# Two ScalarE passes for one of VectorE's in eight early slots, masks on GpSimd, and output pairs from slot 8, in a fused attention and SMELU kernel

## The chip, the cores and the metric

The kernel runs on one core of one Trainium2 chip. The metric is the device time of one execution in microseconds; the time of a kernel is the median of its runs.

## What is computed

Sliding-window attention over 8 batches, 8 heads, 576 positions and head size 64 gives 4608 rows of 512; these go through a feed-forward layer of width 2048 with the SMELU activation.

```python
scores = (q @ k.T) / sqrt(64)                       # kept where |i - j| <= 32
attn   = softmax(scores) ;  x = attn @ v            # x: [4608, 512]
h = x @ w_in                                        # w_in: [512, 2048]
g = h if h >= 1 else 0 if h <= -1 else (h + 1)**2 / 4
out = g @ w_out                                     # w_out: [2048, 512]
```

The kernel uses a form of g without branches. With rr = relu((h + 1)/2), g = min(rr, 1) * max(h, rr). The changed kernel has a second form of it, g = min(max(h, 1), rr * rr), since rr * rr is (h + 1)^2/4 for h over -1 and is at least h everywhere.

## The kernel before, in words

The feed-forward layer is cut into 18 row blocks of 256 rows (TB) by 8 column blocks of 256 hidden columns, in all 144 slots, numbered a in the loop at L462: t is the row block, f the column block. A slot does this, in the order of the code, which is the order in every engine's queue (the schedule is written by hand, L73):

- TensorE makes the hidden block hp in PSUM by 8 matmuls of 128x128 by 256 (L484). It reads xT, the attention's transposed output, and w_in. Slots 6 and 7 take their hp from the pool of the output tiles (L479), all others from ps_h, which has two buffers.
- ScalarE writes rr by a Relu (L488), VectorE writes mx by a max of hp and rr (L490) and gT by min and multiply (L491). hp is free when the max is done.
- run(a) (L498) does the attention work that the dictionary ev has for this slot; then come the output matmuls of `post` (L499), and run(a + 0.5) for attention work that stands behind them.

Output matmuls of the first two row blocks go by pairs (L432): a pair is 8 matmuls of 256 columns, two row tiles by four of the 16 column blocks, and eight pairs fill the output columns of one half. Which slots have which pair is the list `pairs` (L374) up to pair 7; after that slot a takes number a - 8 (L465). From number 16 on it is a quarter (L417), 4 matmuls of 512 columns, as long as a pair in TensorE time. ScalarE copies a finished output tile to osb (L429, L445), and SyncE stores it.

Attention is done per batch and ahead of its rows. `tposes` (L319) transposes q and k of batches 1 and 2 on TensorE into PSUM tiles, two of them per call; ScalarE and VectorE each copy a part of each out (L186). `scores` (L207) makes the scores, ScalarE takes their Exp (L231). The band mask is put in either by matmuls of a bias ahead of the scores (add_mask, L199), if eng is None, which is so below slot 14 (L464), or by a multiplication with mask4 or mask8 on VectorE after the Exp (L197). `sums` (L261) multiplies by v and by ones; ScalarE makes the reciprocal by Ln and Exp (L295, L296), and VectorE's multiplication (L301, L304) puts the result into xT. ps_s and ps_n, the PSUM pools of scores and sums, have one buffer each. `seq` holds the steps of batches 1 to 7, and `at` lays them on slots (L395 to L406). Row block 2 (slots 16 to 23) is the first that reads rows of batch 1.

mask4 and mask8 are copied from band on VectorE at slot 10 (L493). Loads are issued by GpSimd in the order of the code (L121 to L151): w_in in column pieces, then w_out's column half 0 in two row halves, q, k and v of batch 1, w_out's column half 1, and batch 2. In the built program each of GpSimd's loads waits for the one eight before it.

Of the kernel before, what the change touches and what calls it, by code (L numbers as in the profile page):

```python
# [9 lines left out]
AF = mybir.ActivationFunctionType  # L10
ALU = mybir.AluOpType
# [3 lines left out]
def kernel(  # L15
# [21 lines left out]
    NT, DM, DFF = out.shape[0], 512, 2048  # L37
# [4 lines left out]
    TAIL = S - MAIN  # L42
# [13 lines left out]
    ps_s = ctx.enter_context(tc.tile_pool(name="ps_s", bufs=1, space=bass.MemoryType.PSUM))  # L56
# [7 lines left out]
    band = const.tile([128, 192], BF, name="band")  # L64
    bias = const.tile([128, 192], BF, name="bias")
    mask4 = const.tile([128, 8 * 128], BF, name="mask4")
    mask8 = const.tile([128, 4 * TAIL], BF, name="mask8")
# [6 lines left out]
    V, P, A = nc.vector, nc.gpsimd, nc.scalar  # L74


    qn, kn, vn = {}, {}, {}

    def load_half(half, t, h, eng=None, x=None):

        src, dst, nm = ((q, qn, "qh"), (k, kn, "kh"))[t]
        if (0, half) not in dst:
            dst[0, half] = early.tile([128, 2, S], BF, name=nm, tag=nm, bufs=2) if x is None else x
        (eng or nc.gpsimd).dma_start(out=dst[0, half][:, h], in_=src[0].rearrange(
            "(h y) (l p j) d -> h l p y (j d)", h=2, l=2, p=32)[h][half])
# [7 lines left out]
    def load_nat(b, t):  # L93
        src, dst, nm = ((q, qn, "qn"), (k, kn, "kn"))[t]
        x = dst[b] = nat.tile([128, NU, 2, D], BF, name=nm, tag=nm)
        for h in range(2):
            nc.gpsimd.dma_start(out=x[:, :, h], in_=src[b, NY * h:NY * h + NY].rearrange("y s d -> (y s) d")  # L97
                                .rearrange("(u p) d -> p u d", p=128))

    def load_v(b, n):  # L100
        if b not in vn:
            vn[b] = nat.tile([128, 2 * NC, 2, D], BF, name="vn", tag="vn", bufs=3)
        h, a = divmod(n, 2)
        y = NY * h + 2 * a
        nc.gpsimd.dma_start(out=vn[b][64 * a:64 * a + 64, :, h], in_=v[b, y:y + 2].rearrange("y s d -> (y s) d")  # L105
                            .rearrange("(c r) d -> r c d", r=64))
# [35 lines left out]
    def put(todo):  # L142
        for fn, *x in todo:
            fn(*x)

    w = [(load_w_in, c, c + 256, h) for c in range(0, 1024, 256) for h in range(2)]
    w += [(load_w_in, c, c + 512, h) for c in range(1024, DFF, 512) for h in range(2)]
    put(w[:4] + [(load_half, 1, t, h) for t in range(2) for h in range(2)] + w[4:])
    put([(load_w_out, 0, n) for n in range(2)] + [(load_rows, 1, t) for t in range(2)])
    put([(load_v, 1, n) for n in range(4)] + [(load_w_out, 1, n) for n in range(2)])  # L150
    put([(load_rows, 2, t) for t in range(2)] + [(load_v, 2, n) for n in range(4)])  # L151
# [4 lines left out]
    def qkT(b, t):  # L156
# [2 lines left out]
        if b not in kT:  # L159
            kT[b] = ktp.tile([128, NY * S], BF, name="kT")  # L160
        return kT[b]

    HD = (slice(0, 64), slice(64, 128))

    def tpose(b, n, t, copy, ps):

# [13 lines left out]
        for j in range(j0, j1):  # L180
            if isinstance(src, list):
                for h in range(2):
                    nc.tensor.transpose(ps[HD[h], j - j0], src[h][:, D * j:D * j + D], ident)  # L183
            else:
# [3 lines left out]
    def xpose(b, t):  # L188

        nc.sync.dma_start_transpose(out=qkT(b, t).rearrange("d (u p) -> d u p", p=128),  # L190
                                    in_=(qn, kn)[t][b].rearrange("p u h d -> p (u h d)"))
# [7 lines left out]
    def add_mask(ps, n, w):  # L199
        for a in range(2):  # L200
            for h in range(2):
                nc.tensor.matmul(ps[h][HD[a], :n * w].rearrange("p (n j) -> p n j", n=n), ident[HD[h], HD[h]],
                                 bias[HD[h], 64 * h:64 * h + w].rearrange("p (n j) -> p n j", n=1)
                                 .to_broadcast([64, n, w]),
                                 start=True, stop=False, skip_group_check=True)

    def scores(b, ys, pars, cs, eng, pool=ps_s):  # L207
# [8 lines left out]
        for y1 in range(*ys):  # L216
            for par in range(*pars):
                for c2 in range(*cs):
                    c = 2 * c2 + par
                    for a in range(2):  # L220
                        for h in range(2):
                            s0 = S * (y1 + 2 * a) + 64 * c
                            nc.tensor.matmul(ps[HD[a], h, 128 * n:128 * n + 128], kT[b][HD[h], s0:s0 + 64],  # L223
                                             qTs[b % 3][HD[h], PAD + s0 - 32:PAD + s0 + 96],
                                             start=eng is not None, stop=True, skip_group_check=True)
# [8 lines left out]
    def scores8(b, eng, pool=None):  # L234
# [9 lines left out]
        for y1 in range(2):  # L244
            for a in range(2):
                for h in range(2):
                    s0 = S * (y1 + 2 * a) + MAIN
                    nc.tensor.matmul(ps[h][HD[a], TAIL * y1:TAIL * y1 + TAIL], kT[b][HD[h], s0 + 32:s0 + TAIL],
                                     qTs[b % 3][HD[h], PAD + s0:PAD + s0 + TAIL],
# [57 lines left out]
    def flush():  # L307
        while muls:
            muls.pop(0)()
# [61 lines left out]

    NB = NT // TB
    NF = DFF // 256
    pairs = [(10, 0), (10, 1), (11, 2), (12, 3), (13, 4), (14, 5), (15, 6), (16, 7)]  # L374
    ev = {}

    def at(a, *todo):


        ev.setdefault(a, []).extend(x for x in todo if x)  # L380

    def steps(b, cut):

        for k, (lo, hi) in enumerate(((0, cut), (cut, MAIN))):
            for y1 in range(2):
                yield (sums, b, y1, lo, hi), (scores, b, (y1, y1 + 1), (0, 2), (2 * k, 2 * k + 2))
        yield (sums, b, 0, MAIN, S), (scores8, b)
# [4 lines left out]
    at(4, (sums, 0, 1, TB, MAIN))  # L392
    at(5, (sums, 0, 0, MAIN, S, ps_s))
    seq = [x for b in range(1, B) for x in steps(b, 224)]
    at(15, seq[0][0], (*seq[1][0], ps_s))  # L395
    for n, a in enumerate((18, 20, 22, 27)):
        at(a, seq[2 + n][0])
    for n, a in enumerate((13.5, 14.5, 16, 18, 20, 25, 27)):
        at(a, seq[n][1])
    sl = [30, 32, 35, 39, 42, 45, 49, 52, 56, 59, 62, 65, 69, 73, 77, 81, 84, 88, 92]  # L400
    sl += [96, 99, 103, 106, 110, 113, 116, 120, 124, 128]
    for n, a in enumerate(sl):
        at(a, seq[6 + n][0], seq[7 + n][1] if n < len(sl) - 1 else None)
    for b, *a in ((1, 11.5, 12.5), (2, 19.5, 21.5)):
        for t in range(2):
            at(a[t], (tposes, b, (t, 0), (t, 1)))  # L406
    loads, xps = {}, {}
    for b in range(LONG, B):
        a = sl[5 * (b - 1) - 7] - 17
# [5 lines left out]
    gT, op = {}, {}  # L415
# [33 lines left out]
    def run(pos):  # L449
        todo = []  # L450
        for fn, *x in ev.get(pos, []):
            if fn is sums:
                todo.append(sums(*x))
            elif fn is tposes:
                tposes(*x)
            else:
                pool = (x.pop(),) if x[-1] in (ps_s, ps_n, ps_o) else ()
                fn(*x, eng, *pool)
        for end in todo:
            end()  # L460

    for a in range(NF * NB + NF):  # L462
        t, f = divmod(a, NF)
        eng = None if a < 14 else V  # L464
        post = [x for n, x in pairs if n == a] + [a - NF] * (a >= 2 * NF)  # L465
        for b, x in loads.get(a, []):
            if x < 2:
                load_nat(b, x)
            else:
                for n in range(4):  # L470
                    load_v(b, n)
        if a == 0 or a > 3:
            flush()
        if t < NB:
            if t not in gT:
                gT[t] = gtp.tile([128, 2 * NF, TB], BF, name="gT", tag="gT")
            r0 = TB * t % RING
            if a in (6, 7):
                hp = ps_o.tile([128, 2, TB], FP, name="hp", tag="op")  # L479
            else:  # L480
                hp = ps_h.tile([128, 2, TB], FP, name="hp", tag="hp")
            for j in range(2):
                for n, kk in enumerate((0, 2, 1, 3)):
                    nc.tensor.matmul(hp[:, j], w_in[:, kk, 256 * f + 128 * j:256 * f + 128 * j + 128],  # L484
                                     xT[:, kk, r0:r0 + TB], start=n == 0, stop=n == 3)

            rr = ewp.tile([128, 2, TB], FP, name="rr")
            A.activation(rr, hp, AF.Relu, scale=0.5, bias=0.5)  # L488
            mx = ewp.tile([128, 2, TB], FP, name="mx")
            V.tensor_max(mx, hp, rr)  # L490
            V.scalar_tensor_tensor(gT[t][:, 2 * f:2 * f + 2], rr, 1.0, mx, op0=ALU.min, op1=ALU.mult)  # L491
        flush()
        if a == 10:  # L493
            for h in range(2):
                for m, n, w in ((mask4, 8, 128), (mask8, 4, TAIL)):
                    V.tensor_copy(m[HD[h]].rearrange("p (n j) -> p n j", n=n), band[HD[h], 64 * h:64 * h + w]
                                  .rearrange("p (n j) -> p n j", n=1).to_broadcast([64, n, w]))
        run(a)  # L498
        for x in post:  # L499
            (pair if x < 4 * 4 else quarter)(x)  # L500
        run(a + 0.5)
        for x in xps.get(a, []):
            xpose(*x)
# [30 lines left out]
```

The softmax here doesn't subtract the row's maximum and nothing guards it: scores larger than these inputs give would overflow.

## Time and profile before

The three runs took 316.71, 316.87 and 317.66 us; the median is 316.87. The profiled run has a span of 315.0 us.

| what | before |
|---|---|
| TensorE matmuls, busy | 298.4 us, 95% |
| VectorE, busy | 250.8 us, 80% |
| ScalarE, busy | 192.1 us, 61% |
| hidden matmuls L484 | 149.3 us busy in 1152 |
| output matmuls L424, L440 | 123.0 and 16.3 us busy in 477 and 128 |
| Relu L488, mean | 595 ns |
| max L490 and multiply L491, mean | 690 and 692 ns |
| mask copies on VectorE, L496 | 1.19 us from 35.40 us |
| chain of waits that ended last | 86% TensorE, 5% VectorE, 5% ScalarE |

The profile is of one execution. Times count from the start of the span. Engines are PE (TensorE's matmuls), PEld (its weight loads, beside them), DVE (VectorE), ACT (ScalarE), POOL (GpSimd) and SP (SyncE). In the timeline a row is a start, a duration, the engine, the line, the operation with its tiles, and in brackets the idle time ahead of it and what ended that. The ends of matmuls are modelled, so that consecutive ones overlap in the rows; start-to-start times are the safer ones. An instruction that waits for several things is put down to one of them, and where the engine named had long been done it was another.

### The profile page before, as it was taken

How to read it: one execution, taken by the hardware profiler on the slowest of the kernel's cores; microseconds unless marked ns; L12 is line 12 of the kernel's file. 1: busy time of each engine (PE TensorE's matmuls, PEld its weight loads, DVE VectorE, ACT ScalarE, POOL GpSimd, SP SyncE). 2: the span in 40 equal slices, each digit the busy share in tenths (PEclk: the TensorE clock that was granted, in tenths of full speed). 3: DMA queues.
4: the chain of work that ended last, by engine and by line, in shares of the span. 5: the costliest groups of instructions: out<-in, count | busy, mean ns of one | idle time of the engine just before them, and what ended most of it. 6: DMA issues, size and time to landing. Idle time of an engine off the chain costs nothing.

```text
span 315.0 us, 8563 instructions
## 1 busy us (share of the span) xinstructions
PE 298.4 (95%) x3670; PEld 207.7 (66%) x3707; DVE 250.8 (80%) x393; ACT 192.1 (61%) x316; POOL 69.5 (22%) x83
## 2 busy tenths in 40 slices
PE   8987998999999999999999999999999999999995
PEld 3566877776666666666666666666666666667652
DVE  4279986877988888888888888888888888878760
ACT  3677375765765776567756666566676666654431
POOL 8784354652060406040503000000000000000000
PEclk9999999999999999999999999999999999999999
DMA  9999999999999969997993983005501100100111
GB/s 151 185 199 202 174 215 174 164 169 166 168 167 117 107 141 167 101 91 123 173 127 54 90 127 95 33 35 111 108 35 35 36 33 35 36 33 35 42 60 67
DMA packets 123558, 34.54 MB, mean 110 GB/s; under 512 B 108160, under 2 KB 119168, under 8 KB 123520
## 3 DMA queue, kind: packets, MB, share of 16 engines
q0 software_dynamic: 94176, 18.06, 74.1%
q1 hardware_dynamic: 29200, 15.63, 19.7%
q8 instruction: 29, 0.48, 0.6%
q10 hardware_dynamic: 144, 0.29, 0.4%
q14 instruction: 9, 0.07, 0.1%
HBM read 36.70 MB, written 9.44 MB: 146 GB/s over the span
## 4 chain that ended last, share of the span: by engine, by line
PE 86%; DVE 5%; ACT 5%; issue 3%; ACTq 0%
PE hp L484 37%; PE op L424 35%; PE bb L289 5%; PE op L440 4%; PE bb L223 2%; PE z L332 2%; DVE mx L490 2%; ACT pt L231 1%; ACT rc L296 1%; DVE gT L491 1%; PE tp L183 1%; DVE xT L301 1%; ACT lr L295 1%; DVE kT L186 1%; DVE qT L186 1%
## 5 line engine op out<-in xcount | busy, mean ns | idle before, releaser
L484 PE MATMUL hp<-xT,w_in 128*128 128x256 bf16 x1152 | 149.3, 273 | 4.0 <-DVE mx L490 1.9
L488 ACT ACTIVATE rr<-hp 128x512 f32<-128x512 f32 x144 | 85.7, 595 | 92.5 <-PE hp L484 91.1
L484 PEld LDWEIGHTS <-w_in 128*128 128x128 bf16 x1152 | 111.8, 98 | 44.2 <-issue 5.0
L424 PE MATMUL op<-w_out,gT 128*128 128x512 bf16 x477 | 123.0, 379 | 5.0 <-issue 4.8
L490 DVE TENSOR_TENSOR mx<-hp,rr 128x512 f32<-128x512 f32 x144 | 99.3, 690 | 33.7 <-ACT rr L488 31.5
L491 DVE SCALAR_TENSOR_TENSOR gT<-rr,mx 128x512 bf16<-128x512 f32 x144 | 99.6, 692 | 4.9
L424 PEld LDWEIGHTS <-gT 128*128 128x128 bf16 x512 | 47.6, 98 | 36.7
L231 ACT ACTIVATE pt<-bb 128x1024 bf16<-128x1024 f32 (+1 forms) x33 | 33.2, 1012 | 5.4 <-PE bb L223 4.0
L105 POOL DMA_DIRECT2D vn<-in_v_dram x32 | 27.3, 867 | 40.7 <-PE bb L223 36.2
L301 DVE TENSOR_TENSOR xT<-bb,rc 128x512 bf16<-128x512 f32 (+1 forms) x32 | 21.1, 658 | 11.1 <-ACT rc L296 10.4
L429 ACT COPY osb<-op 128x512 f32<-128x512 f32 x32 | 18.7, 583 | 11.5 <-PE op L424 11.1
L296 ACT ACTIVATE rc<-lr 128x512 f32<-128x512 f32 (+2 forms) x40 | 23.6, 589 | 1.3
L295 ACT ACTIVATE lr<-bb 128x512 f32<-128x512 f32 (+2 forms) x40 | 22.0, 551 | 0.8 <-PE bb L289 0.7
L97 POOL DMA_DIRECT2D qn<-in_q_dram x10 | 12.2, 1222 | 43.9 <-DMA qT<-qn 37.5
L289 PE MATMUL bb<-pt,ones 64*64 64x256 bf16 (+3 forms) x352 | 19.6, 255 | 1.9 <-DVE kT L186 0.8
L197 DVE TENSOR_TENSOR pt<-pt,mask 128x1024 bf16<-128x1024 bf16 (+1 forms) x34 | 21.0, 616 | 0.2 <-ACT pt L231 0.2
L289 PE MATMUL bb<-pt,vn 64*64 64x128 bf16 (+3 forms) x712 | 18.5, 204 | 0.2 <-issue 0.2
L289 PEld LDWEIGHTS <-ones 64*64 64x64 bf16 x352 | 10.4, 105 | 10.4 <-issue 10.4
L289 PEld LDWEIGHTS <-vn 64*64 64x64 bf16 x712 | 16.8, 107 | 0.3 <-issue 0.3
L440 PE MATMUL op<-w_out,gT 128*128 128x256 bf16 x128 | 16.3, 273 | 0.0
L97 POOL DMA_DIRECT2D kn<-in_k_dram x10 | 12.1, 1213 | 9.7 <-PE tp L183 3.9
L440 PEld LDWEIGHTS <-gT 128*128 128x128 bf16 x128 | 12.1, 98 | 1.7
(53 smaller groups left out, 107.8 us busy)
## 6 DMA issues: line engine op xcount, KB each, us to landing
out_dram<-osb SPq DMA_DIRECT2D x36, 256.0 KB, 2.3
vn<-in_v_dram POOLq DMA_DIRECT2D x32, 144.0 KB, 8.2
qn<-in_q_dram POOLq DMA_DIRECT2D x10, 288.0 KB, 7.7
kn<-in_k_dram POOLq DMA_DIRECT2D x10, 288.0 KB, 8.8
w_out<-in_moe_w_out_dram POOLq DMA_DIRECT2D x4, 512.0 KB, 13.2
qn<-in_q_dram POOLq DMA_DIRECT2D x2, 576.0 KB, 14.7
kn<-in_k_dram POOLq DMA_DIRECT2D x2, 576.0 KB, 15.7
w_in<-in_moe_w_in_dram POOLq DMA_DIRECT2D x8, 128.0 KB, 5.4
```

What stands on the lines that cost most here:

```text
L97: nc.gpsimd.dma_start(out=x[:, :, h], in_=src[b, NY * h:NY * h + NY].rearrange("y s d -> (y s) d") .rearrange("(u p) d -> p u d", p=128))
L105: nc.gpsimd.dma_start(out=vn[b][64 * a:64 * a + 64, :, h], in_=v[b, y:y + 2].rearrange("y s d -> (y s) d") .rearrange("(c r) d -> r c d", ...
L231: A.activation(p, ps[:, :, :128 * n].rearrange(like, y=m), AF.Exp, scale=D ** -0.5)
L289: nc.tensor.matmul(bb[HD[h], a, o + c0:o + c1], ones[HD[a]] if c is None else vn[b][HD[a], c, h], p(a, h), start=n == 0, stop=True, skip_g ...
L295: A.activation(lr[:, :, :D0], bb[:, :, D0:2 * D0], AF.Ln)
L296: A.activation(rc[:, :, :D0], lr[:, :, :D0], AF.Exp, scale=-1.0)
L424: nc.tensor.matmul(o, gT[tt // 2][:, j, 128 * (tt % 2):128 * (tt % 2) + 128], w_out[:, j], start=not done, stop=len(done) == 2 * NF - 1, s ...
L440: nc.tensor.matmul(o[:, tt], gT[p][:, j, 128 * tt:128 * tt + 128], w_out[:, j, 256 * half:256 * half + 256], start=not done, stop=len(done ...
L484: nc.tensor.matmul(hp[:, j], w_in[:, kk, 256 * f + 128 * j:256 * f + 128 * j + 128], xT[:, kk, r0:r0 + TB], start=n == 0, stop=n == 3)
L488: A.activation(rr, hp, AF.Relu, scale=0.5, bias=0.5)
L490: V.tensor_max(mx, hp, rr)
L491: V.scalar_tensor_tensor(gT[t][:, 2 * f:2 * f + 2], rr, 1.0, mx, op0=ALU.min, op1=ALU.mult)
```

## The change

The activation of slots 1, 2 and 7 to 12 takes its square on ScalarE and leaves one pass, max and min, to VectorE. The masks are copied by GpSimd, once for all 128 partitions, after band's lower half has been shifted in place; these copies stand behind the w_in loads and ahead of the w_out loads. The last 512 columns of w_in are loaded in four pieces instead of two. Output pairs begin at slot 8, one a slot up to slot 13; slot 14 has none, slot 15 has two. Batch 1's transposes stand ahead of the pair of slots 11 and 12 instead of behind it; its first scores are at 13 and 13.5 instead of 13.5 and 14.5, and its first sums at slot 14 instead of 15. It is for filling TensorE's idle time in these slots and taking load off VectorE there.

```diff
     w = [(load_w_in, c, c + 256, h) for c in range(0, 1024, 256) for h in range(2)]
-    w += [(load_w_in, c, c + 512, h) for c in range(1024, DFF, 512) for h in range(2)]
+    w += [(load_w_in, 1024, 1536, h) for h in range(2)]
+    w += [(load_w_in, c, c + 256, h) for c in range(1536, DFF, 256) for h in range(2)]
     put(w[:4] + [(load_half, 1, t, h) for t in range(2) for h in range(2)] + w[4:])
+    P.tensor_copy(band[HD[1], 0:128], band[HD[1], 64:192])
+    for m, n, x in ((mask4, 8, 128), (mask8, 4, TAIL)):
+        P.tensor_copy(m.rearrange("p (n j) -> p n j", n=n),
+                      band[:, :x].rearrange("p (n j) -> p n j", n=1).to_broadcast([128, n, x]))
...
-    pairs = [(10, 0), (10, 1), (11, 2), (12, 3), (13, 4), (14, 5), (15, 6), (16, 7)]
+    pairs = [(8, 0), (9, 1), (10, 2), (11, 3), (12, 4), (13, 5), (15, 6), (15, 8), (16, 7), (17, 9)]
+    two_on_act = (1, 2, 7, 8, 9, 10, 11, 12)
...
-    at(15, seq[0][0], (*seq[1][0], ps_s))
+    at(14, seq[0][0], (*seq[1][0], ps_s))
...
-    for n, a in enumerate((13.5, 14.5, 16, 18, 20, 25, 27)):
+    for n, a in enumerate((13, 13.5, 16, 18, 20, 25, 27)):
...
-    for b, *a in ((1, 11.5, 12.5), (2, 19.5, 21.5)):
+    for b, *a in ((1, 11, 12), (2, 19.5, 21.5)):
...
-        post = [x for n, x in pairs if n == a] + [a - NF] * (a >= 2 * NF)
+        post = [x for n, x in pairs if n == a] + [a - NF] * (a >= 2 * NF + 2)
...
             A.activation(rr, hp, AF.Relu, scale=0.5, bias=0.5)
+            g = gT[t][:, 2 * f:2 * f + 2]
             mx = ewp.tile([128, 2, TB], FP, name="mx")
-            V.tensor_max(mx, hp, rr)
-            V.scalar_tensor_tensor(gT[t][:, 2 * f:2 * f + 2], rr, 1.0, mx, op0=ALU.min, op1=ALU.mult)
+            if a in two_on_act:
+                A.activation(mx, rr, AF.Square)
+                V.scalar_tensor_tensor(g, hp, 1.0, mx, op0=ALU.max, op1=ALU.min)
+            else:
+                V.tensor_max(mx, hp, rr)
+                V.scalar_tensor_tensor(g, rr, 1.0, mx, op0=ALU.min, op1=ALU.mult)
         flush()
-        if a == 10:
-            for h in range(2):
-                for m, n, w in ((mask4, 8, 128), (mask8, 4, TAIL)):
-                    V.tensor_copy(m[HD[h]].rearrange("p (n j) -> p n j", n=n), band[HD[h], 64 * h:64 * h + w]
-                                  .rearrange("p (n j) -> p n j", n=1).to_broadcast([64, n, w]))
         run(a)
```

More of the change, by code (lines that the diff above doesn't have):

```diff
@@ L77 @@
     qn, kn, vn = {}, {}, {}
+    HD = (slice(0, 64), slice(64, 128))
     def load_half(half, t, h, eng=None, x=None):
@@ L161, in qkT @@
         return kT[b]
-    HD = (slice(0, 64), slice(64, 128))
     def tpose(b, n, t, copy, ps):
```

## The prediction

> **What bounds the kernel now.** I read the page's busy totals first, then the windows view cut into stages, then the timeline of all engines where the stages leave TensorE time unused, and last the timeline of GpSimd, whose queue the change lengthens. The page (busy totals, and the share of the DMA engines in 40 slices of 7.9 us) and the windows view (columns: window, length, then busy time with instruction counts for PE, PEld, DVE, ACT, POOL):
>
> ```profile
> PE 298.4 (95%) x3670; PEld 207.7 (66%) x3707; DVE 250.8 (80%) x393; ACT 192.1 (61%) x316; POOL 69.5 (22%) x83
> DMA  9999999999999969997993983005501100100111
> ...
> 13.80:28.90 15.10, 12.58 (x239) 9.47 (x237) 11.51 (x19) 11.10 (x21) 10.65 (x14) 1.00 1.34 199
> 28.90:52.85 23.95, 21.38 (x316) 17.41 (x316) 20.26 (x34) 14.34 (x22) 9.90 (x11) 1.00 1.67 194
> 75.00:303.50 228.50, 223.58 (x2590) 154.10 (x2622) 195.18 (x296) 141.96 (x236) 24.76 (x24) 1.00 0.69 89
> ```
>
> From 75 us on TensorE is the bound: a slot is 0.87 us of hidden matmuls (L484) plus 0.86 us of output matmuls (L424) and the chain of waits runs through them without a break. That work is fixed, so a microsecond gained before 75 us moves the end by a microsecond. The stage that the change edits is slots 8 to 16, 28.90 to 52.85 us. Its TensorE work by start-to-start times: 9 hidden blocks x 0.87, 9 output pairs x 0.87, two transpose sets x 1.13, scores 0.57 (with mask matmuls) + 0.35 + 0.35, sums 1.04: 20.2 us. So 3.7 of 23.95 us are lost. The timeline says where:
>
> ```profile
> 28.30 0.55 DVE L304 TENSOR_TENSOR xT<-bb,rc 128x384 bf16<-128x384 f32 x1
> 28.76 0.68 DVE L490 TENSOR_TENSOR mx<-hp,rr 128x512 f32<-128x512 f32 x1
> 28.90 1.91 PE L484 MATMUL hp<-xT,w_in 128*128 128x256 bf16 x16 [1.05 <-DVE xT L304]
> ...
> 32.15 1.03 PE L484 MATMUL hp<-xT,w_in 128*128 128x256 bf16 x8 [1.34 <-DVE mx L490]
> 35.40 1.19 DVE L496 COPY mask<-band 64x1024 bf16<-64x1024 bf16 x4
> ...
> 47.25 0.29 PE L289 MATMUL bb<-pt,ones 64*64 64x224 bf16 x4 [0.39 <-DVE pt L197]
> 49.12 0.38 PE L484 MATMUL hp<-xT,w_in 128*128 128x256 bf16 x2 [0.33 <-DVE xT L301]
> 50.00 0.81 PE L484 MATMUL hp<-xT,w_in 128*128 128x256 bf16 x6 [0.51 <-DVE xT L301]
> ```
>
> VectorE runs without a gap from 24.57 to about 40 us. It is late with xT (L304), then with the buffer of slot 10 (30.64 to 32.15, 1.5 us with the modelled matmul ends removed), and slots 15 and 16 wait for batch 1: 0.4 for the mask, 0.5 and 0.7 for xT. That is 3.1; the rest is some 0.1 us at each switch between full and quarter tiles. Loads:
>
> ```profile
> 17.22 0.62 POOL L109 DMA_DIRECT2D w_in<-in_moe_w_in_dram  x1 [0.15 <-issue]
> 17.82 1.79 POOL L114 DMA_DIRECT2D w_out<-in_moe_w_out_dram  x2
> ...
> 27.83 0.89 POOL L114 DMA_DIRECT2D w_out<-in_moe_w_out_dram  x1 [1.06 <-DMA w_out<-in_moe_w_out_dram]
> ```
>
> Issue times plus the DMA view's times to landing give: last w_in 17.2+7.8=25.0, w_out halves 27.5 and 30.2, batch 1's qn 33.1, kn 36.0, vn 37.5 to 40.2, second w_out column half 42.6 and 46.4. They land one behind another at the DMA row's 9s: this stream sets landings, not GpSimd's issue.
>
> [...] the trace has 690 (L490) and 692 (L491), so fusing two VectorE passes into one saves a whole 0.69. [...] the trace has 595 for Relu and 589 for an SBUF-to-SBUF Exp. I price Square at 0.60; before has none. The built kernel still has one table load. [...]
>
> **The change part by part.**
> *Squares, slots 1, 2.* Slot 1's Square (16.95 to 17.55) pushes ScalarE's copies back 0.55, but VectorE, one pass lighter, starts its own copies behind them: kT is done at 19.7, not 20.09. Slot 2's matmuls, shown waiting for a mx done earlier, really wait for w_in, issued near 12.1 and 6.0 long: 18.19 stays. Relu 19.26 to 19.86, Square to 20.45, so the first Exp starts at 20.45 for 20.61. ScalarE is back to back from there to 28.48, so everything through xT (L304) moves by 0.15: slot 8 starts at 28.73.
> *Squares, slots 7 to 12.* ScalarE has per slot 1.2 for 0.6, VectorE 0.69 for 1.38. The hidden buffer is now held for 0.60+0.60+0.69 us, about 1.95 with hand-offs, in place of 1.3. Two buffers and slots of 1.74 us (hidden block plus pair) cover it: slot 10 needs slot 8's, free at 29.8+1.9=31.6, and comes at 32.2. The 1.5 us stall goes and pairs 0 and 1 fill it.
> *Pairs from slot 8.* Ledger of starts: hidden 8 at 28.73, pair 0 29.6, 9 at 30.5, pair 1 31.3, 10 at 32.2, pair 2 33.1, 11 at 33.95, q transposes 34.9, pair 3 36.05, 12 at 36.9. Loads needed: w_out 27.5 and 30.2, qn 33.1, all landed. ScalarE: Square 11 ends at 36.2, two q copies (0.7 each) to 37.6, osb copy to 38.2, Relu and Square 12 to 39.4, two k copies to 40.8. VectorE's copies stand behind ScalarE's (a wait in the built program), q done 38.35, k done 41.55. So k transposes 37.8 to 38.95, pair 4 to 39.8, hidden 13 to 40.7.
> *Batch 1 a slot sooner.* Scores at 13 stand ahead of pair 5 in TensorE's queue and wait for the k copies: 41.55, a new stall of some 0.6, ending 41.9. Behind them queue pair 5, the next scores and hidden 14. Pair 5 to 42.85; the second scores wait for the first Exp (42.05 to 43.05) because their pool has one buffer, 0.2 more; they add mask matmuls (0.57 for 0.35) and end at 43.65. Hidden 14 to 44.55, sums 44.65 to 45.65 with no VectorE mask wait, hidden 15 to 46.5, pairs 6 and 8 to 48.25. Meanwhile ScalarE: Relu 14 to 45.3, Ln and Exp twice at 0.57 to 47.6; VectorE's second xT to 48.2. Hidden 16 thus has no wait: 48.25 to 49.1; scores to 49.55; pair 7 needs gT of slot 15, done 49.5, and ends at 50.45.
> Hidden 17 starts at 50.45 for 52.85, with the same pairs done: 2.4 us. From there both queues are the same in order, and the engines' backlogs relative to TensorE are alike.
> *Masks.* VectorE loses 1.19 us at slot 10 (already in the ledger). GpSimd copies 128+1024+384=1536 elements per partition. Low end: the 257-element select at L131 took 0.44 us, 1.7 ns each: 2.6. [...] I take 3.
> *Split w_in.* Two more issues of 0.62 and the copies delay the w_out issue from 17.8 to about 22.2 (the last two w_in also wait for loads eight before, near 18). [...] The ledger leaves 0.7 before qn and kn are needed (33.1 against 34.9; 36.0 against 37.8 less the slip), and 1.1 before pair 0. I cost it at nothing: hidden by slots 8 to 10. The split itself makes slot 6's weights land before 25.0; slot 6 started at 25.93, so no gain.
> Sum: 0.15 before slot 8, 2.25 in slots 8 to 16. 316.87-2.4=314.5.
>
> **Rivals.** *ScalarE becomes the bound in slots 11 to 14.* From 29.7 to 41.5 us it has 10.0 of 11.8 us filled (five slots of 1.2, four copies of 0.7, osb and Relu 13 at 0.6). If hand-offs add 0.1 to each of twelve dependent passes, k copies and both Exps come 1.2 later and hold hidden 14: gain 1.2, 315.7. For it: ScalarE is the tightest engine of my ledger; against: Ln to Exp is 0.62 start to start in the trace, only 0.03 over its busy time.
> *The loads starve (slower).* If the copies take 10 us [...], w_out is issued at 29, the stream slips 7 us, pair 0 goes from 29.6 to 34.5 and TensorE's in-order queue with it: 4.9-2.4 = 2.5 lost, 319.4. [...] With 7 us the slip is 4, the loss 1.9, the time 316.4, no change.
> *The gain is given back after slot 17.* The chain of waits has VectorE's transpose copies at 60.71 (1.28 us) and 66.94 (1.38 us). If these kept their clock times, whatever holds them, TensorE would wait for them and all 2.4 would be lost: 316.9, no change. Against: they follow TensorE's own transposes, which come earlier with it, and the loads these read landed by 52.1 (kn issued 36.30, 15.8 on its way).
>
> **How the numbers follow.** Ledger 0.64 (314.5 +-0.8), ScalarE bound 0.16 (315.7), gain given back or a part starved 0.12 (316.4 to 316.9), starved or otherwise worse 0.08 (319.4). Faster by over 0.3% is below 315.9: nearly all of the first and most of the second, 0.79; slower 0.09; same 0.12. The low end takes away the 0.6 us stall at slot 13 and the 0.2 behind it: 313.6. The high end reaches the mildest of the third case, 316.4, and leaves the last 0.2 out.
>
> **What would show it.** Right: hidden 10 with no wait for VectorE, the first block after the second half of xT with none, hidden 17 near 50.5 us, a new wait of TensorE for the k copies near 41 us, stages after 53 us unchanged in length. Wrong: TensorE waiting for w_out, qn or kn loads; Squares well over 0.6 or a second table load; GpSimd copies above 5 us; the 22.15 us that now follow slot 17's start (52.85 to 75.00) longer than they are.

## The result and the profile after

| kernel | median us | lowest to highest | runs |
|---|---|---|---|
| before | 316.85 | 316.71 to 317.66 | 4 |
| after | 315.04 | 314.94 to 315.19 | 4 |

The ratio is 0.9938, with a 95% interval of 0.9921 to 0.9955: faster by 0.6%, or 1.81 us. The prediction had 314.5 (2.4 us) with a range from 313.6 to 316.4. The profiled execution of after took 315.10 us and its span, from the first to the last instruction in the profile, is 313.0; that of before took 316.82 with a span of 315.0.

The changed kernel is five lines longer, so hidden matmuls are now L489, pairs L445, Relu L493, the new Square L497, the new max-and-min pass L498, max L500, multiply L501, sums L293 and the two halves of xT L305 and L308. Busy totals and DMA row of the page of after:

```profile
PE 304.1 (97%) x3711; PEld 207.9 (66%) x3711; DVE 243.7 (78%) x380; ACT 196.2 (63%) x324; POOL 72.3 (23%) x88
...
DMA  9999999999999989896996792006501000100111
```

VectorE loses 7 us, ScalarE gains 4. TensorE's busy time is not to be read as more work: of its 5.7 us, 4.9 lie from 73 us on, where the work is the same and only 34 more of its matmuls are on record (2624 for 2590). The windows view of after, cut at slot 8, at slot 17 and at about the places where the prediction had cut (columns as before: window, length, busy time and count for PE, PEld, DVE, ACT, POOL):

```profile
29.40:50.81 21.41, 21.24 (x321) 17.55 (x321) 13.66 (x21) 16.34 (x27) 9.06 (x10) 1.00 1.66 195
50.81:73.00 22.19, 20.66 (x333) 16.91 (x331) 18.10 (x29) 15.10 (x26) 14.04 (x14) 1.00 2.48 165
73.00:301.50 228.50, 228.50 (x2624) 154.17 (x2622) 195.08 (x296) 141.81 (x236) 24.80 (x25) 1.00 0.79 91
```

Slots 8 to 16 take 21.41 us where they took 23.95. TensorE's timeline of after shows how:

```profile
29.40 1.03 PE L489 MATMUL hp<-xT,w_in 128*128 128x256 bf16 x8 [1.17 <-DVE xT L308]
30.27 1.04 PE L445 MATMUL op<-w_out,gT 128*128 128x256 bf16 x8
31.14 1.04 PE L489 MATMUL hp<-xT,w_in 128*128 128x256 bf16 x8
32.01 1.04 PE L445 MATMUL op<-w_out,gT 128*128 128x256 bf16 x8
32.89 1.04 PE L489 MATMUL hp<-xT,w_in 128*128 128x256 bf16 x8
...
41.80 0.66 PE L227 MATMUL bb<-qT,kT 64*64 64x128 bf16 x16
42.39 1.05 PE L445 MATMUL op<-w_out,gT 128*128 128x256 bf16 x8
43.58 0.41 PE L206 MATMUL bb<-bias,ident 64*64 64x512 bf16 x4
...
48.60 1.04 PE L489 MATMUL hp<-xT,w_in 128*128 128x256 bf16 x8
...
50.81 1.04 PE L489 MATMUL hp<-xT,w_in 128*128 128x256 bf16 x8
```

Hidden 10 (32.89) and hidden 16 (48.60) have no wait, and blocks and pairs alternate 0.87 us apart. So the stage did better than the 2.25 us forecast: it gave 2.54. Why then did the whole give less? The stage lengths of the two profiles, from the start of slot 0, 8 and 17 in the timelines:

| | before | after | change |
|---|---|---|---|
| start of the span to slot 0 | 14.01 | 14.96 | +0.95 |
| slots 0 to 7 | 14.89 | 14.44 | -0.45 |
| slots 8 to 16 | 23.95 | 21.41 | -2.54 |
| slot 17 to the end | 262.15 | 262.19 | +0.04 |
| span | 315.0 | 313.0 | -2.0 |
| time outside the span | 1.8 | 2.1 | +0.3 |
| time of this execution | 316.82 | 315.10 | -1.72 |

Most of the loss lies ahead of slot 0, where the change touches nothing on TensorE, and the experiments start there. The 0.3 us outside the span come up again with the masks.

### The profile page after: what moved, and what is told of

Same layout as the page of the kernel before. It is cut to its first block, busy times and chain, and to the rows that moved or that the text cites. A ratio compares the mean times of both kernels' runs of the same rounds, so it can differ in the third digit from the quotient of the medians.

```text
span 313.0 us, 8615 instructions
## 1 busy us (share of the span) xinstructions
PE 304.1 (97%) x3711; PEld 207.9 (66%) x3711; DVE 243.7 (78%) x380; ACT 196.2 (63%) x324; POOL 72.3 (23%) x88
## 4 chain that ended last, share of the span: by engine, by line
PE 90%; ACT 4%; DVE 3%; issue 1%; ACTq 0%
PE hp L489 38%; PE op L429 36%; PE bb L293 6%; PE op L445 4%; PE bb L227 2%; PE z L336 2%; ACT pt L235 2%; PE tp L187 1%; DVE xT L305 1%; ACT rc L300 1%; ACT lr L299 1%; DVE kT L190 1%; DVE qT L190 1%; DVE mx L500 1%; ACT rr L493 0%
## 5 line engine op out<-in xcount | busy, mean ns | idle before, releaser
L489 PE MATMUL hp<-xT,w_in 128*128 128x256 bf16 x1152 | 149.3, 273 | 2.0 <-DVE xT L308 1.2
L493 ACT ACTIVATE rr<-hp 128x512 f32<-128x512 f32 x144 | 85.6, 595 | 87.1 <-PE hp L489 86.2
L489 PEld LDWEIGHTS <-w_in 128*128 128x128 bf16 x1152 | 112.0, 98 | 41.6 <-issue 2.6
L429 PE MATMUL op<-w_out,gT 128*128 128x512 bf16 x512 | 130.4, 380 | 0.0
L500 DVE TENSOR_TENSOR mx<-hp,rr 128x512 f32<-128x512 f32 x136 | 93.7, 689 | 33.2 <-ACT rr L493 31.3
L501 DVE SCALAR_TENSOR_TENSOR gT<-rr,mx 128x512 bf16<-128x512 f32 x136 | 94.1, 692 | 4.6
L429 PEld LDWEIGHTS <-gT 128*128 128x128 bf16 x512 | 47.5, 98 | 36.8
L305 DVE TENSOR_TENSOR xT<-bb,rc 128x512 bf16<-128x512 f32 (+1 forms) x32 | 21.0, 657 | 11.0 <-ACT rc L300 10.3
L293 PE MATMUL bb<-pt,ones 64*64 64x256 bf16 (+3 forms) x352 | 19.5, 255 | 1.5 <-DVE kT L190 0.8
L201 DVE TENSOR_TENSOR pt<-pt,mask 128x1024 bf16<-128x1024 bf16 (+1 forms) x33 | 20.2, 613 | 0.1
L293 PE MATMUL bb<-pt,vn 64*64 64x128 bf16 (+3 forms) x712 | 18.2, 204 | 0.0
L293 PEld LDWEIGHTS <-ones 64*64 64x64 bf16 x352 | 10.2, 105 | 9.9 <-issue 9.9
L293 PEld LDWEIGHTS <-vn 64*64 64x64 bf16 x712 | 16.7, 107 | 0.0
L445 PE MATMUL op<-w_out,gT 128*128 128x256 bf16 x128 | 16.5, 273 | 0.0
L227 PE MATMUL bb<-qT,kT 64*64 64x128 bf16 x520 | 13.2, 217 | 0.3 <-DVE kT L190 0.2
## 6 DMA issues: line engine op xcount, KB each, us to landing
qn<-in_q_dram POOLq DMA_DIRECT2D x2, 576.0 KB, 13.5
```

The costliest lines, as they stand in the source:

```text
L293: nc.tensor.matmul(bb[HD[h], a, o + c0:o + c1], ones[HD[a]] if c is None else vn[b][HD[a], c, h], p(a, h), start=n == 0, stop=True, skip_g ...
L429: nc.tensor.matmul(o, gT[tt // 2][:, j, 128 * (tt % 2):128 * (tt % 2) + 128], w_out[:, j], start=not done, stop=len(done) == 2 * NF - 1, s ...
L445: nc.tensor.matmul(o[:, tt], gT[p][:, j, 128 * tt:128 * tt + 128], w_out[:, j, 256 * half:256 * half + 256], start=not done, stop=len(done ...
L501: V.scalar_tensor_tensor(g, rr, 1.0, mx, op0=ALU.min, op1=ALU.mult)
```

## The experiments

Differences in time below are against the repeat of the changed kernel (314.44 us), differences in stages against its profile (14.52 us for slots 0 to 7, 21.40 for slots 8 to 16), unless another is named. The kernels ran in three sets, in which before took 317.45, 317.39 and 317.4 us, so that their times can be set side by side. In the set of the first pair it took 316.85; its single executions lie between 316.67 and 317.86 in all four.

### The same kernel again, and a shorter warm-up

The rows of the first matmuls (L336, L332 in before; a warm-up that works on a dummy tile) differ between the two profiles: 6.11 us after, 5.15 before. The repeat is the changed kernel with no edit. The other kernel has:

```diff
-    keep_warm(14, ps_h, "hp")
+    keep_warm(11, ps_h, "hp")
```

> The changed kernel again, to learn how much of its start varies. In the profiles TensorE's first 14 warm-up matmuls took 5.15 us before and 6.11 us after the change, from the same code, and slot 0 began 0.95 us later. Theory CLOCK [...]: other executions of this kernel have fewer slow warm-up matmuls, so its times spread over up to 1 us and this profile shows the warm-up anywhere from 5.1 to 6.2 us. Theory PROGRAM (the changed program itself starts late): again 6.1 us, slot 0 near 14.96 us, times within 0.2 us of 315.0.

> The changed kernel with 11 instead of 14 warm-up matmuls at the start, nothing else. If the late start comes from slow warm-up matmuls standing in TensorE's queue ahead of the first transposes (14 x 0.425 us = 5.95), 11 of them end at 1.19 + 4.68 = 5.9 us, when the first transposes' input is ready: slot 0 begins 0.4 to 0.9 us sooner and the time is 314.1 to 314.6. If [...] the start is late for another reason, no change from 315.0.

Measured: the repeat 314.44 us (314.24 to 314.72), ratio to before 0.9912 (0.9895 to 0.9928), before in that set 317.45; with 11 warm-up matmuls 314.52 (314.33 to 314.86), ratio 0.9915 (0.9898 to 0.9931). TensorE's timeline of before, of after, and then of the repeat:

```profile
1.19 5.15 PE L332 MATMUL z<-warm 128*128 128x512 bf16 x14 [1.19 <-DVE warm L126]
...
14.01 0.38 PE L484 MATMUL hp<-xT,w_in 128*128 128x256 bf16 x2
```

```profile
1.19 6.11 PE L336 MATMUL z<-warm 128*128 128x512 bf16 x14 [1.19 <-DVE warm L127]
...
14.96 0.38 PE L489 MATMUL hp<-xT,w_in 128*128 128x256 bf16 x2
```

```profile
1.19 4.59 PE L336 MATMUL z<-warm 128*128 128x512 bf16 x14 [1.19 <-DVE warm L127]
...
14.02 0.38 PE L489 MATMUL hp<-xT,w_in 128*128 128x256 bf16 x2
...
28.54 1.03 PE L489 MATMUL hp<-xT,w_in 128*128 128x256 bf16 x8 [0.95 <-DVE xT L308]
```

The same 14 instructions of the same program took 6.11 and 4.59 us, and the repeat's slot 0 starts at 14.02, as before's does. Its span is 312.1: 2.9 us under before's 315.0, with the same start. That is the effect of the change on the span; in the first pair of profiles 0.95 of it was taken off by the start. In time these two executions, 316.82 and 314.24 us, are 2.58 apart. The medians, 317.45 and 314.44, are 3.01 apart, but the median execution of before is 0.6 us longer than its profiled one, and no trace shows why. Later profiles agree on how the warm-up row and slot 0 hang together:

| warm-up row, us | 4.59 | 5.15 (before) | 5.46 | 5.64 | 6.07 | 6.11 |
|---|---|---|---|---|---|---|
| slot 0 starts at | 14.02 | 14.01 | 14.32 | 14.50 | 14.93 | 14.96 |

Above some 5.15 us every further microsecond of warm-up is one of slot 0; below it slot 0 stays between 14.00 and 14.14, in the profiles left out of the table too. That is why 11 warm-up matmuls (a row of 4.08 us, slot 0 at 14.03) gained nothing on the repeat, whose start wasn't late; slots 0 to 7 took 14.91 us in that profile. It is 0.5 us under after's 315.04, whose start was late. The pace of the matmuls makes the difference: their weight loads come about 0.43 us apart throughout in after; in the repeat they do up to 3.73 us, and the last six, from 4.10 us on, come 0.22 apart. What sets the moment is not shown. The mean granted clock is 1.0 in after's profile and 0.999 in the repeat's; that a clock sets the pace, as the name of theory CLOCK says, was the author's guess. What the runs bear out is its forecast, a row that varies from execution to execution.

### Before, once more

No edit.

> The kernel before once more, one profile. Theory CLOCK: its 14 warm-up matmuls take some other time than the 5.15 us of its first profile, anywhere from 4.6 to 6.1 us, and slot 0 starts at 14.0 to 15.0 us accordingly; from slot 8 to slot 17 it takes the same 23.95 us, and from slot 17 to the end the same 262.2 us. Theory PROGRAM: again 5.15 us and slot 0 at 14.01.

Measured: 316.78 us, span 315.0. TensorE's timeline:

```profile
1.19 4.69 PE L332 MATMUL z<-warm 128*128 128x512 bf16 x14 [1.19 <-DVE warm L126]
```

The row differs from the first profile's 5.15 us, as theory CLOCK had it, and is too short to hold slot 0 back. Slot 0 starts at 14.00, slot 8 at 28.86, slot 17 at 52.81: stages of 14.86 and 23.95 us, as in the first profile of before. Against the repeat the stages give 0.34 and 2.55.

### Without the Squares, and with two of them

```diff
-    two_on_act = (1, 2, 7, 8, 9, 10, 11, 12)
+    two_on_act = ()
```

The second kernel has (1, 2) in place of the empty tuple.

> The changed kernel with the old form of the activation in all slots (no Squares); masks, pairs, loads and batch 1 as changed. Theory FILL (the stall of slot 10 went because a pair now lies between two hidden blocks, 1.74 us a slot against VectorE's 1.38): within 0.5 us of the changed kernel, 315.0 to 315.5, hidden 10 with no wait. Theory RELIEF (the stall went because VectorE has one pass for two, as the prediction's sum had it): TensorE waits for VectorE again in slots 8 to 12 and the time is 316.3 or more.

> The changed kernel with Squares in slots 1 and 2 alone; slots 7 to 12 have the old form. If the Squares' whole worth (0.35 us, from the run without any) comes from slots 1 and 2, where they let the early transposes' copies and scores start sooner: 314.3 to 314.6, as the repeated changed kernel (314.44). If those of slots 7 to 12 are worth it: 314.8, as without any.

Measured: without Squares 314.79 us (314.54 to 315.29), ratio 0.9923 (0.9908 to 0.9938); with those of slots 1 and 2 alone 314.69 (314.08 to 315.22), ratio 0.9913 (0.9898 to 0.9929). TensorE's timeline without Squares:

```profile
19.90 0.41 PE L206 MATMUL bb<-bias,ident 64*64 64x512 bf16 x4 [0.81 <-DVE qT L190]
...
29.26 1.03 PE L489 MATMUL hp<-xT,w_in 128*128 128x256 bf16 x8 [1.31 <-DVE xT L308]
...
32.75 1.04 PE L489 MATMUL hp<-xT,w_in 128*128 128x256 bf16 x8
```

Hidden 10, at 32.75, has no wait though VectorE does two passes in every slot again, and slots 8 to 16 take 21.43 us (also 21.43 with two Squares). So the six Squares of slots 7 to 12 are worth nothing that shows.

Those of slots 1 and 2 do show in slots 0 to 7. Without them the scores behind slot 2 wait for VectorE's copy of qT and start 5.51 to 5.52 us after slot 0, in this profile as in both of before, and slots 0 to 7 take 14.86 to 14.89 us. With them the scores start 5.02 to 5.06 after slot 0 and the stage takes 14.44 to 14.56 in six profiles of this study (after, the repeat and four others; the last kernel below isn't counted, as its edit changes this stage). So the two Squares are worth 0.3 to 0.45 us there, if w_in lands in time: in four more profiles with Squares slot 2 started over 4.2 us after slot 0, its scores followed late, and the stage took 14.74 to 15.18. In time the 0.35 us between the medians can't be told from the spread, as the unchanged kernel gave 315.04 and 314.44. The kernel with two Squares is one of the four, with a load in the way again at slot 4:

```profile
23.82 1.03 PE L489 MATMUL hp<-xT,w_in 128*128 128x256 bf16 x8 [1.21 <-DMA w_in<-in_moe_w_in_dram]
```

Slots 0 to 7 took 15.18 us there, with 1.21 us of waiting for w_in at slot 4; and its 314.69 us lies between what was expected for either answer. It says nothing on slots 1 and 2.

### Without the earlier pairs

```diff
-    pairs = [(8, 0), (9, 1), (10, 2), (11, 3), (12, 4), (13, 5), (15, 6), (15, 8), (16, 7), (17, 9)]
+    pairs = [(10, 0), (10, 1), (11, 2), (12, 3), (13, 4), (14, 5), (15, 6), (16, 7)]
-        post = [x for n, x in pairs if n == a] + [a - NF] * (a >= 2 * NF + 2)
+        post = [x for n, x in pairs if n == a] + [a - NF] * (a >= 2 * NF)
```

> The changed kernel with the output pairs where they were before (two in slot 10, then one a slot); Squares, masks, loads and batch 1 as changed. Theory FILL: hidden 10 then waits for slot 8's buffer, held by Relu, Square and one VectorE pass until about 31.6, with no pair to do; 1.4 us of pairs left undone at that point, some of which fills the waits at 13 and 13.5: 0.9 to 1.4 us slower than the changed kernel, 315.3 to 315.9. Theory RELIEF (the lighter VectorE alone removes the stall of slot 10): within 0.3 us of the changed kernel.

Measured: 316.17 us (316.01 to 316.54), ratio 0.9963 (0.9949 to 0.9977), 1.73 us slower and above the range expected; slots 8 to 16 take 22.76 us, 1.36 more, and slot 0 starts 0.48 later in this profile. TensorE's timeline:

```profile
28.94 1.91 PE L489 MATMUL hp<-xT,w_in 128*128 128x256 bf16 x16 [1.31 <-DVE xT L308]
...
32.05 1.03 PE L489 MATMUL hp<-xT,w_in 128*128 128x256 bf16 x8 [1.20 <-DVE gT L498]
```

Hidden blocks 8 and 9 stand next to each other again and hidden 10 waits 1.20 us for a buffer, now for the one pass that Squares leave to VectorE. It frees the buffer hardly sooner than before's max did, which stood behind two passes for each earlier slot: hidden 10 comes 3.11 us behind hidden 8, and in before 3.25. So the pairs remove the stall, and the Squares do not.

### Batch 1's attention in its old place

```diff
-    at(14, seq[0][0], (*seq[1][0], ps_s))
+    at(15, seq[0][0], (*seq[1][0], ps_s))
-    for n, a in enumerate((13, 13.5, 16, 18, 20, 25, 27)):
+    for n, a in enumerate((13.5, 14.5, 16, 18, 20, 25, 27)):
-    for b, *a in ((1, 11, 12), (2, 19.5, 21.5)):
+    for b, *a in ((1, 11.5, 12.5), (2, 19.5, 21.5)):
```

> The changed kernel with batch 1's transposes, first scores and first sums in the slots they had before (11.5, 12.5; 13.5, 14.5; 15). The prediction's ledger: the waits of the first block of row block 2 for xT come back (0.5 + 0.7 us, and 0.4 for the mask), the new waits at 13 and 13.5 (measured 0.25 + 0.3) and the 0.24 us of mask matmuls go: 0.7 to 0.9 us slower than the changed kernel, 315.8 to 316.0. Rival (the two pairs now in slot 15 already cover the wait for xT): within 0.3 us of the changed kernel.

Measured: 315.66 us (315.27 to 315.73), ratio 0.9947 (0.9933 to 0.9961), 1.22 us slower. Slots 8 to 16 take 21.89 us, 0.49 more, and their wait is back:

```profile
46.88 0.29 PE L293 MATMUL bb<-pt,ones 64*64 64x224 bf16 x4 [0.71 <-DVE pt L201]
```

The sums wait for the mask's multiplication, as in before. Slot 16, at 49.13, starts without a wait for xT, though before waited twice there: the two pairs of slot 15 cover it, as the rival had it, and the stage loses less than the 0.7 to 0.9 expected. The other 0.7 us lie in slots 0 to 7 (15.18 us for 14.52), where the two programs are alike on TensorE; the profile has a wait of 1.00 us at slot 4 there, of the size that the kernel with two Squares had for w_in. Whether this comes with the edit or with the execution is not settled.

### The masks: on VectorE, and four times over on GpSimd

The first kernel puts the copies back on VectorE:

```diff
-    P.tensor_copy(band[HD[1], 0:128], band[HD[1], 64:192])
-    for m, n, x in ((mask4, 8, 128), (mask8, 4, TAIL)):
-        P.tensor_copy(...)
+        if a == 10:
+            for h in range(2):
+                for m, n, w in ((mask4, 8, 128), (mask8, 4, TAIL)):
+                    V.tensor_copy(...)
```

The second has GpSimd write both masks four times:

```diff
-    for m, n, x in ((mask4, 8, 128), (mask8, 4, TAIL)):
+    for m, n, x in ((mask4, 8, 128), (mask8, 4, TAIL)) * 4:
```

> The changed kernel with the masks copied by VectorE at slot 10, as before. VectorE idles about 1.06 us in each of slots 8 to 11 now, so 1.19 us of copies there should delay one pass by 0.2 at most, with no one waiting for it: within 0.2 us of the changed kernel, 314.3 to 314.7. Rival (the mask copies were on the path through VectorE to the q copies): 0.5 to 1.2 us slower.

> The changed kernel with GpSimd's two mask copies made four times over (the result is the same), 4.5 us more ahead of the w_out loads. Theory HIDDEN WITH A MARGIN: the w_out issue goes from about 20.6 to 25.1 us, the stream of loads runs dry and w_out lands near 30.5, some 2.6 us later than now; pair 0 stands at 29.4, so 1.0 to 1.5 us are lost, 315.4 to 315.9, with TensorE waiting for w_out at pair 0. Rival (the stream never starves, landings are set by bandwidth alone): within 0.2 us. Rival (no margin): the whole 2.6 us or more, 317.

Measured: on VectorE 314.38 us (314.26 to 314.74), ratio 0.9906 (0.989 to 0.9922), slots 8 to 16 in 21.39 us: no difference there. Fourfold 317.50 (316.66 to 318.77), ratio 1.0011 (0.9998 to 1.0023), 3.06 us slower. GpSimd's timeline of after, and of the fourfold kernel:

```profile
19.59 0.29 POOL L151 COPY band<-band 64x128 bf16<-64x128 bf16 x1
19.94 1.49 POOL L153 COPY mask<-band 128x1024 bf16<-128x1024 bf16 x2
21.37 1.77 POOL L115 DMA_DIRECT2D w_out<-in_moe_w_out_dram  x2
```

```profile
19.51 6.25 POOL L153 COPY mask<-band 128x1024 bf16<-128x1024 bf16 x8
25.71 1.77 POOL L115 DMA_DIRECT2D w_out<-in_moe_w_out_dram  x2
```

TensorE's timeline of the fourfold kernel:

```profile
31.66 1.05 PE L445 MATMUL op<-w_out,gT 128*128 128x256 bf16 x8 [1.72 <-DMA w_out<-in_moe_w_out_dram]
```

The three copies of after take 1.78 us to the next issue. Each further two copies took 1.6 us; with w_out issued 4.3 us later (25.71 for 21.37) pair 0 waits 1.72 us for w_out and slots 8 to 16 take 23.49, 2.09 more. The loss expected was 1.0 to 1.5. The profiled execution took 316.74 us, 2.5 over the repeat's; half of the 22 executions took 317.96 or more, and what they lost beyond it has no trace. This is the second rival of the prediction made true, so the way it would have failed was the right one to fear, and after stays clear of it.

One effect of the masks' move lies outside the traces. Time less span is 1.7 to 1.85 us in every execution of before whose span is on record and of the kernel with the masks on VectorE, and 1.95 to 2.2 in all executions of kernels with GpSimd's copies, one set or four. The profile of the masks on VectorE and that of after show it in a pair: slot 0 at 14.93 and 14.96, span 313.0 in both, 314.74 and 315.10 us in time. So the move gains nothing in the stages and costs some 0.3 us of time outside the span; what takes it isn't shown.

### w_in's last columns in two pieces

```diff
-    w += [(load_w_in, 1024, 1536, h) for h in range(2)]
-    w += [(load_w_in, c, c + 256, h) for c in range(1536, DFF, 256) for h in range(2)]
+    w += [(load_w_in, c, c + 512, h) for c in range(1024, DFF, 512) for h in range(2)]
```

> The changed kernel with the last 512 columns of w_in in two loads, as before, not four. Slot 6 has its weights in time either way (25.0 against 25.7 us), so by the ledger within 0.3 us of the changed kernel (314.1 to 314.8). Rival: slots 6 and 7 wait for w_in, or the w_out loads come 1.2 us sooner and something gains: 0.4 us or more either way.

Measured: 315.01 us (314.13 to 315.15), ratio 0.9919 (0.9905 to 0.9933); stages of 14.74 and 21.41 us. The median lies outside the expected range, but its runs spread over a microsecond and take in the repeat's, so the split is worth nothing that these runs can show, and a gain of 0.6 us, the difference of the medians, isn't excluded.

### Two stalls that both kernels have

Past slot 17 two waits are left, in the repeat as in before. TensorE's timeline of the repeat:

```profile
59.12 0.30 PE L293 MATMUL bb<-pt,ones 64*64 64x256 bf16 x4 [0.77 <-DVE qT L190]
...
65.45 0.28 PE L293 MATMUL bb<-pt,ones 64*64 64x192 bf16 x4 [0.77 <-DVE kT L190]
```

These are the sums of slots 20 and 22. Putting them behind the slot's pair gives TensorE the pair's 0.87 us to do meanwhile:

```diff
-    for n, a in enumerate((18, 20, 22, 27)):
+    for n, a in enumerate((18, 20.5, 22.5, 27)):
-    for n, a in enumerate((13, 13.5, 16, 18, 20, 25, 27)):
+    for n, a in enumerate((13, 13.5, 16, 18, 20.5, 25, 27)):
```

A last kernel has this and, for the wait of slot 8 for xT (0.95 us in the repeat), lets VectorE do batch 0's last xT before slot 5's multiplication:

```diff
-                V.scalar_tensor_tensor(g, rr, 1.0, mx, op0=ALU.min, op1=ALU.mult)
+                if a != 5:
+                    V.scalar_tensor_tensor(g, rr, 1.0, mx, op0=ALU.min, op1=ALU.mult)
...
         run(a)
+        if a == 5:
+            muls.append(lambda g=g, rr=rr, mx=mx: V.scalar_tensor_tensor(g, rr, 1.0, mx, op0=ALU.min, op1=ALU.mult))
```

> The changed kernel with batch 1's later sums (and the scores of its tail) behind the output pair in slots 20 and 22 (20.5 and 22.5) instead of ahead of it. In the profile TensorE waits there 0.8 us each for the transpose copies of batch 2. If the pair fills these waits: 1.0 to 1.6 us faster than the changed kernel, 312.8 to 313.5. Rival: the waits move to the next transposes and hidden blocks, less than 0.4 us gained.

> As the run before it, and VectorE's multiplication of slot 5 (gT) put behind batch 0's last xT in its queue, so that slot 8 waits less for that xT. VectorE does this gT in the 0.6 us right before the xT, whose inputs are ready by then: a further 0.5 to 0.6 us, 312.3 to 312.9, with TensorE's wait at slot 8 down from 1.0 to some 0.4 us. Rival (ScalarE's Ln and Exp set the moment, not VectorE's queue): no further gain.

Measured: the moved sums 313.22 us (312.95 to 313.65), ratio 0.9873 (0.9858 to 0.9888), with neither wait in the profile; both edits 312.87 (312.74 to 313.66), ratio 0.9863 (0.9848 to 0.9878). TensorE's timeline with both:

```profile
26.00 3.02 PE L489 MATMUL hp<-xT,w_in 128*128 128x256 bf16 x24
29.19 1.03 PE L445 MATMUL op<-w_out,gT 128*128 128x256 bf16 x8 [0.17 <-DVE mx L500]
...
37.98 1.20 PE L187 MATMUL tp<-ident,kn 128*64 128x128 bf16 x36 [0.21 <-DMA kn<-in_k_dram]
```

The first edit gives 1.22 us of the 1.54 that waited. The second nearly takes slot 8's wait away: hidden blocks 6 to 8 are one row, within which slot 8 starts at 27.99, 0.23 us late, and so 0.66 sooner than with the first edit alone (28.65). But its profile spans 310.8 us as that of the first alone: the gain is spent on short new waits behind it, of pair 0 for a max (0.17 idle) and of batch 1's transposes, those of k for a load that doesn't move (0.21). Its 0.35 us in time lie within the spread of the two. This kernel is 1.4% under before and is the fastest of the study.

## Why the prediction was right, and where it was off

**Faster, by the slots 8 to 16: right.** The sum had 2.25 us there, and 2.55 came (repeat against the second profile of before). Its ledger, counted from slot 8's start, against after:

| step | ledger, us | after, us |
|---|---|---|
| hidden 10 | 3.5 | 3.49 |
| hidden 12 | 8.2 | 8.21 |
| pair 5 (behind the first scores) | 13.2 | 12.99 |
| hidden 14 | 14.9 | 14.75 |
| hidden 15 | 16.9 | 16.57 |
| hidden 17 | 21.7 | 21.41 |

The 0.3 us is made at the scores of slot 13. The ledger had a stall of 0.6 for VectorE's k copies and 0.2 for the pool with one buffer, 0.8 in all. The rows at 41.80 and 43.58 give 0.24 (0.59 to the next row where 16 such matmuls take 0.35) and 0.32 (1.19 behind a pair of 0.87), together 0.56; and the sums took 0.85 in place of 1.0.

**"The 1.5 us stall goes and pairs 0 and 1 fill it": half right.** It goes, and it is the pairs that do it: 1.36 us without them, and hidden 10 waits 1.20 with all Squares in place. The step before that, in which the Squares' holding time of "about 1.95 with hand-offs, in place of 1.3" was weighed against slots of 1.74, is right as arithmetic: it shows that Squares make a buffer's hold longer and that spacing covers it (in after 1.98 us from the Relu's start to the end of the last read of hp in slot 8, and 1.32 in slot 13, which has no Square). What the prediction failed to draw from it is that the Squares of slots 7 to 12 then bring nothing; slots 8 to 16 are 21.43 us without them.

**"0.15 before slot 8": undersized.** The term measured 0.34 (repeat against the second profile of before), and 0.44 between after and the profile without Squares. The prediction held slot 2's start at 18.19 and Square's end at 20.45. In the repeat slot 2 starts at 18.05, after 0.62 us of waiting for w_in, and the first Exp at 20.29. The way was right: VectorE's lighter queue lets the scores start sooner (5.02 us after slot 0 for 5.51), and ScalarE then sets the Exp, which follows the Square with no idle time; in before ScalarE sat idle for 0.75 us ahead of it.

**The start and the time outside the span, of which nothing was said: the terms that were missing.** With the starts alike the change takes 2.9 us from the span (315.0 to 312.1). The sum of 2.4 was 0.5 short. The profiled execution of after then lost 0.95 ahead of slot 0 and 0.3 outside the span. These errors pull in opposite directions, and that 315.04 came out so near 314.5 is in part luck. That the other runs of that set, with spans of 312.8 to 313.1, started late too is likely but was only argued: they have no trace.

**Batch 1 sooner.** Hidden 16 has no wait, as forecast, but with batch 1 in its old place it has none either, so what goes with this step is the wait for the mask. It is worth 0.49 us in its stage. What the rest of its 1.22 us is stays open. Nor do the single undoings of pairs (1.36) and batch 1 (0.49) add up to the 2.55 of the stage: before lacked both, and what each is worth without the other wasn't tried.

**Costed at nothing.** GpSimd's copies were priced at 3 us, of which the 1.7 ns per element of the trace's select give 2.6 and the rest was the author's estimate; they took 1.78. The slip that the ledger allows the loads was an estimate as well. GpSimd's third w_out issue, which waits for w_out to land, came at 27.83 us in before, 27.93 in the repeat and 29.37 in after. w_out, qn and kn land in time: no row of TensorE names them in after. The masks' move, costed at nothing, cost the 0.3 us outside the span. The Square took 0.63 for 0.60, the pass of max and min 0.69, and the table load stayed single (1.28 us, from 1.41 us). The stage after slot 17 is 262.19 for 262.15, so nothing is given back, and ScalarE, with Square 0.63 behind each Relu and no row of TensorE waiting for it, did not become the bound.

## What to carry to other kernels

Here a stall of the matmul engine for a buffer was filled by putting other ready matmuls between two uses of the buffer: hidden 10 waits for nothing. A pass less on VectorE did not do it, as 1.20 of the 1.34 us stayed. Doing one of the two without the other shows which it was. When an effect under study is near a microsecond, compare stages from the first row of real work, because the start has a spread of its own (14.00 to 14.96 us in these profiles), and set each execution's time beside its span, because a change can also cost time that no stage has (some 0.3 us here). GpSimd's computing among its load issues cost no stage anything while the landing that it delayed had slack (1.78 us of copies), and 2.09 us in slots 8 to 16 when it was longer than that (the fourfold copies): work that slack out from the issue, and test it by making the work longer.

## What the runs showed that was not expected

- The same 14 warm-up matmuls take 4.59 to 6.11 us in different executions, and the start of the real work moves by up to 0.95 us with them, half as much as the spans of the first two profiles differ.
- With the mask copies on GpSimd an execution's time exceeds its span by 1.95 to 2.2 us, without them by 1.7 to 1.85.
- Loads of the first 25 us land with a spread of their own: slot 4 waited 0.23 us for w_in in the first profile of after, not at all in the repeat, and 1.21 in the kernel with two Squares.
- GpSimd's copy of 1408 elements of bf16 per partition took 1.49 us, 1.06 ns each, and that of 128 took 0.29. The prediction's low end for these copies, taken from the select of 257 elements in 0.44 us, was 1.7 ns each.
